# Padding the two tiles of the softmax sums from 48 to 256 bytes per partition

## The chip, the core and the metric

One core of a Trainium2 chip runs the whole program. The metric is the time of one execution on the device in microseconds; smaller is better. The engines are TensorE (PE in the rows, its weight loads PEld), VectorE (DVE), ScalarE (ACT), GpSimd (POOL) and SyncE (SP), which here issues nearly all DMA transfers. SBUF is the on-chip memory of 128 partitions; a tile takes the same range of bytes in each of its partitions, so one number, the byte at which it starts, says where it lies.

## What is computed

Attention in which a query sees only the keys of its own hash bucket, and two multilayer blocks on its output, in single precision:

```
q_bucket = bits(q @ proj > 0);  k_bucket = bits(k @ proj > 0)     # 6 bits each
scores = where(q_bucket == k_bucket, q @ k.T / 8, -1e9)           # 2 x 8 heads, 768 x 768, depth 64
p = exp(scores - max(scores));  attn = (p / (sum(p) + 1e-9)) @ v
x = attn as 1536 tokens x 512
h = max(x @ w1, x @ w2, x @ w3) @ w_out                           # 512 -> 768 -> 512
g = where(y >= 1, y, where(y <= -1, 0, (y + 1)**2 / 4)), y = h @ w_in
out = g @ w_out2                                                  # 512 -> 2048 -> 512
```

## The kernel before

**Attention** (to about 235 us) goes through 96 tiles of 128 queries. For each tile TensorE makes scores of 768 keys (lines 374 and 377: `lo` by `qa`, then `hi` by `qb`), VectorE copies them to a tile `p` and finds the extreme (384), ScalarE takes the exponential in place and writes the row sums to one column of the tile `sums` (396), TensorE transposes the six blocks of `p` (404, against the identity `ident`), ScalarE or VectorE copies them out to `pt` (413), and after three tiles TensorE multiplies `pt` by the values `vr` (422). A pair of heads has one tile `sums` of 12 columns; two such tiles take turns (`bufs=2` of the pool `nm`). At the end of a pair VectorE turns the sums into reciprocals (465, 466), TensorE transposes them (469), and the normalised result is written to `x_hl` as a high and a low part.

**The multilayer blocks** (from about 235 us, with their first few products already inside attention) are three loops over products of 128 x 128 weights with 512 columns, each made of three passes of high and low parts: `l1` and the loop behind it (both through the helper `mm3`, line 708), `l3` (line 708 too) and `l4` (line 835). `l3` and `l4` take turns, twelve products of one and twelve of the other. A weight slice is loaded by DMA to `wr`, taken apart by ScalarE, VectorE and GpSimd by way of `wg` and `wg2`, and put into one of seven buffers that are used in rotation: five named `w` and, once attention has given back its memory, two named `wx`.

In a product one operand is loaded into the array first (the stationary one, `lhsT`) and the other is streamed through it (the moving one, `rhs`). At line 708 the weights `w` or `wx` are stationary and `x_hl` or `hh` moves; at line 835 `g` is stationary and the weights `w` or `wx` move. In attention, `qa`, `qb`, `p` and `vr` are stationary and `lo`, `hi`, `ident` and `pt` move.

**Where the tiles lie.** Pools are placed one behind the other in the order in which they are opened, a tile's size being rounded up to 32 bytes. The pool `nm` opens behind the constants, `x_hl`, the weight buffers and the tiles `h`, and its first two tiles are `sums`. They take 48 bytes each, so 64 with rounding, and 128 together. Everything ahead of them ends at a multiple of 256; everything behind them that has a size of a multiple of 256 therefore begins 128 bytes past one:

| tiles | start of the first, bytes | past a multiple of 256 |
|---|---|---|
| `ident`, `x_hl`, `wr`, `wg`, `wg2`, `w`, `h` | 18432 (`ident`), 18944 (`x_hl`), 84480 (`w`) | 0 |
| `sums` | 111104 and 111168 | 0 and 64 |
| `u`, `uc`, `uo`, `rt`, `rb`, `xr`, `r` | 111232 (`u`) | 128 |
| `hi`, `lo`, `qa`, `qb`, `vr`, `p`, `pt` | 136320 (`hi`) | 128 |
| `wx`, `hh`, `acc`, `g` and the `r` of the multilayer blocks | 130176 (`wx`), 138368 (`hh`), 162944 (`g`) | 128 |
| `nm` (four of 4 bytes), `z` | 205440, 205568 | 128 to 224, 0 |
| `pj_st`, two parts | 16960, 17392 | 64, 240 |

The slices that products and transposes take of `x_hl`, `w`, `wx`, `hh`, `g`, `p`, `pt`, `vr` and the like begin a multiple of 256 bytes into their tile, so a slice lies past a multiple of 256 as its tile does.

Of the kernel before, what the change touches and what calls it, by code (L numbers as in the profile page):

```python
# [8 lines left out]
F32 = mybir.dt.float32  # L9
# [10 lines left out]
NK = S // 128  # L20
# [90 lines left out]
def lsh_attention_moe_kernel(  # L111
# [23 lines left out]
    nm_p = ctx.enter_context(tc.tile_pool(name="nm", bufs=2))  # L135
# [113 lines left out]
    def attention(mlp_steps):  # L249
        with ExitStack() as ax, ExitStack() as sx:  # L250
# [10 lines left out]
            head, pair, tl, grp = {}, {}, {}, {}  # L261
# [128 lines left out]
            def t_exp(n):  # L390
                h, t = divmod(n, NK)
                if n % (2 * NK) == 0:
                    pair[h // 2] = dict(sums=nm_p.tile([128, 2 * NK], F32, tag="sums", name="sums"))
                p = tl[n]["p"]
                c = (h % 2) * NK + t
                nc.scalar.activation(  # L396
                    out=p, in_=p, func=ACTF.Exp, scale=-1.0, bias=tl[n]["nm"],
                    accum_out=pair[h // 2]["sums"][:, c:c + 1],
                )
# [199 lines left out]
            def tile_tasks(n):  # L599
                h, t = divmod(n, NK)  # L600
                g, r = divmod(n, 3)
                sp, pp = place("s", 1), place("p", 2)
                tb = [place(f"t{i}", 1) for i in range(2)]
                if n % (2 * NK) == 0:
                    sums_p[h // 2] = place("sums", 1)
                if r == 0:
                    pt_p_[g] = place("pt", 1)
                qk = task("PE", 0.75, n, t_qk, n, after=ready[h], takes=[sp], leaves=[h_place[h]])
                mx = task("DVE", 0.97, n, t_max, n, after=[qk], takes=[pp], leaves=[sp])
                ex = task("ACT", 1.06, n, t_exp, n, after=[mx], takes=[sums_p[h // 2]] if n % (2 * NK) == 0 else [], lag=0.1)  # L610
                exps[n] = ex
                outs, tr = [], None
                for half in range(2):
                    tr = task("PE", 0.325, n - 4, t_tr, n, half, after=[ex, tr], takes=[tb[half]], leaves=[pp], lag=0.1)
                    cp = task("ACT", 0.48, n - 2, t_out, n, half, nc.scalar.copy, after=[tr], takes=[pt_p_[g]] if r == 0 and half == 0 else [], leaves=[tb[half]])
                    work.also("DVE", 0.55, lambda a=(n, half, nc.vector.tensor_copy): t_out(*a), cp)
                    outs += [cp]
                return outs
# [34 lines left out]
            for n in range(NT_):  # L653
                h, t = divmod(n, NK)
# [259 lines left out]
```

## Time and profile before

| | us |
|---|---|
| median of 3 runs (704.96 to 705.01) | 704.96 |
| the profiled execution, its own time | 704.98 |
| its span, first to last instruction | 703.2 |
| TensorE busy in the span | 695.2 |
| VectorE, ScalarE, GpSimd busy | 455.5, 374.0, 282.7 |

The profiled execution is 0.02 us from the median and its span 1.8 us shorter than its time. Products overlap in TensorE's pipeline: the duration of one (near 390 ns for 512 columns) is longer than the distance from one to the next, so the pace is read from how many fall in a stretch. A stretch's count has every product of which any part lies in it.

### The profile page before, as it was taken

The numbers are of one execution on the slowest core, as the hardware profiler recorded it, in microseconds if no ns is written. First come the engines' busy times: TensorE is split into PE (matmuls) and PEld (weight loads), VectorE is DVE, ScalarE is ACT, GpSimd is POOL, SyncE is SP. The second block draws the span as 40 slices with busy tenths as digits, with TensorE's granted clock in tenths as the row PEclk, the third lists the DMA queues.
The fourth block names the chain that finished last, engine by engine and source line by source line (L and its number), as shares of the span: only waits on it lengthen the run. The fifth ranks groups of instructions, "written<-read, shape, count | busy, mean of one in ns | idle before, by whom it ended". The sixth has DMA issues, their size and how long they took to land.

```text
span 703.2 us, 9982 instructions
## 1 busy us (share of the span) xinstructions
PE 695.2 (99%) x3548; PEld 553.9 (79%) x3548; DVE 455.5 (65%) x696; ACT 374.0 (53%) x733; POOL 282.7 (40%) x262
## 2 busy tenths in 40 slices
PE   8999999999999999999999999999999999999998
PEld 6777777777777688888888888888888888888886
DVE  6646555666655486775444355765888888888844
ACT  4788898888888423332321233665544444444430
POOL 3555646647523034442332022444344344344330
PEclk9999999999999999999999999999999999999999
DMA  5655557546511222221111022120111122111004
GB/s 164 162 149 151 132 145 202 139 121 167 132 46 45 95 91 90 90 91 52 56 49 54 31 89 90 47 75 31 60 61 61 60 66 84 61 61 60 31 0 180
DMA packets 25658, 62.78 MB, mean 89 GB/s; under 512 B 4085, under 2 KB 9813, under 8 KB 25609
## 3 DMA queue, kind: packets, MB, share of 16 engines
q1 hardware_dynamic: 25576, 62.15, 29.2%
q8 instruction: 28, 0.46, 0.3%
q14 instruction: 22, 0.17, 0.1%
q0 software_dynamic: 32, 0.00, 0.0%
HBM read 42.07 MB, written 3.19 MB: 64 GB/s over the span
## 4 chain that ended last, share of the span: by engine, by line
PE 97%; DVE 1%; issue 0%; DMA 0%; ACT 0%; DVEq 0%; ACTq 0%
PE b L708 47%; PE b L835 19%; PE u_ps L422 10%; PE t_ps L404 9%; PE s_ps L374 5%; PE s_ps L377 5%; PE pj_ps L337 2%; DMA r<-in_kq 0%; DVE p L384 0%; DVE lo L302 0%; DVE qb L344 0%; DVE qa L331 0%; DVE pt L413 0%; PE pj_ps L469 0%; ACT pt L413 0%
## 5 line engine op out<-in xcount | busy, mean ns | idle before, releaser
L708 PE MATMUL b<-x_hl,w 128*128 128x512 f32 (+1 forms) x900 | 203.1, 382 | 0.0
L708 PEld LDWEIGHTS b<-x_hl,w 128*128 128x128 f32 x900 | 164.0, 188 | 34.2 <-issue 0.6
L384 DVE TENSOR_SCALAR_CACHE_REDUCE p<-s_ps 128x768 f32<-128x768 f32 x96 | 91.1, 955 | 43.7 <-PE s_ps L377 32.4
L735 POOL TENSOR_TENSOR g<-r,g 128x512 fp32r<-128x512 f32 x48 | 62.6, 1306 | 125.6 <-ACT g L734 125.6
L835 PE MATMUL b<-w,g 128*128 128x512 f32 (+1 forms) x438 | 108.4, 392 | 0.0
L219 POOL TENSOR_TENSOR w<-wg,w 128x512 fp32r<-128x512 f32 (+1 forms) x42 | 59.4, 1414 | 96.7 <-ACT w L213 80.8
L835 PEld LDWEIGHTS b<-w,g 128*128 128x128 f32 x438 | 81.9, 189 | 18.7
L396 ACT ACTIVATE p<-p,nm 128x768 f32<-128x768 f32 x96 | 89.8, 937 | 9.0 <-DVE p L384 8.5
L192 DVE SCALAR_TENSOR_TENSOR wg<-wg,wr 128x512 f32<-128x512 f32 (+1 forms) x58 | 66.1, 1140 | 36.2 <-ACT wg L190 35.4
L213 ACT CAST w<-wg 128x512 fp32r<-128x512 f32 (+1 forms) x42 | 25.4, 605 | 115.6 <-DVE wg L205 115.6
L708 PE MATMUL b<-x_hl,wx 128*128 128x512 f32 x360 | 86.1, 395 | 0.0
L404 PEld LDWEIGHTS t_ps<-ident,p 128*128 128x128 f32 x576 | 66.5, 140 | 22.7 <-ACT p L396 11.5
L404 PE MATMUL t_ps<-ident,p 128*128 128x128 f32 x576 | 82.1, 276 | 1.1 <-DVE pt L413 0.9
L708 PEld LDWEIGHTS b<-x_hl,wx 128*128 128x128 f32 x360 | 67.9, 189 | 15.8
L413 ACT COPY pt<-t_ps 128x384 f32<-128x384 f32 x158 | 69.5, 480 | 18.2 <-PE t_ps L404 16.3
L374 PE MATMUL s_ps<-lo,qa 128*128 128x384 f32 x192 | 72.3, 377 | 1.0 <-DVE p L384 0.9
L422 PE MATMUL u_ps<-pt,vr 128*64 128x384 f32 x384 | 69.6, 495 | 0.2 <-ACT pt L413 0.2
L377 PE MATMUL s_ps<-hi,qb 76*128 76x384 f32 x192 | 65.3, 340 | 0.2 <-DVE hi L331 0.2
L815 DVE SCALAR_TENSOR_TENSOR r<-r,b 128x512 f32<-128x512 f32 x48 | 33.0, 687 | 48.2 <-ACT r L814 47.8
L842 DVE TENSOR_TENSOR acc<-b,acc 128x512 f32<-128x512 f32 (+1 forms) x85 | 56.5, 676 | 8.0 <-PE b L835 8.0
L813 ACT ACTIVATE r<-b,half_sb 128x512 f32<-128x512 f32 x48 | 32.9, 686 | 46.1 <-PE b L708 40.8
L197 DVE TENSOR_SCALAR wg<-wg 128x512 int32<-128x512 int32 (+1 forms) x58 | 53.9, 929 | 2.8
(80 smaller groups left out, 847.5 us busy)
## 6 DMA issues: line engine op xcount, KB each, us to landing
wr<-in_w SPq DMA_DIRECT2D x50, 512.0 KB, 3.1
r<-in_kq SPq DMA_DIRECT2D x15, 384.0 KB, 3.9
vr<-in_v SPq DMA_DIRECT2D x16, 192.0 KB
rb<-d SPq DMA_DIRECT2D x16, 192.0 KB, 3.3
wr<-in_w SPq DMA_DIRECT2D x8, 384.0 KB, 2.8
qa<-hi SPq DMA_DIRECT2D x15, 192.0 KB
qb<-hi SPq DMA_DIRECT2D x15, 192.0 KB, 4.0
qa<-lo SPq DMA_DIRECT2D x15, 192.0 KB, 2.7
```

What stands on the lines that cost most here:

```text
L192: nc.vector.scalar_tensor_tensor(out=f32(g), in0=f32(g), scalar=TINY_SQ, in1=f32(high), op0=ALU.is_ge, op1=ALU.mult)
L219: nc.gpsimd.tensor_tensor(out=w[:, 1, 0:cols], in0=f32(g2), in1=f32(w[:, 0, 0:cols]), op=ALU.subtract)
L374: nc.tensor.matmul(out=o, lhsT=hd["qa"][:, qs], rhs=hd["lo"][:, ks], start=True, stop=False)
L377: nc.tensor.matmul(out=o, lhsT=hd["qb"][0:76, qs], rhs=hd["hi"][0:76, ks], start=False, stop=True)
L384: nc.vector.tensor_scalar(out=p.rearrange("p (a k) -> p a k", a=2), in0=s_ps[n % 2][:, :, 0:HALF], scalar1=MASKED, scalar2=MASKED, op0=ALU ...
L396: nc.scalar.activation(out=p, in_=p, func=ACTF.Exp, scale=-1.0, bias=tl[n]["nm"], accum_out=pair[h // 2]["sums"][:, c:c + 1],)
L404: nc.tensor.transpose(out=t_ps[half][:, j * 128:(j + 1) * 128], in_=tl[n]["p"][:, kt * 128:(kt + 1) * 128], identity=ident,)
L413: copy(out=grp[g][:, 3 * half:3 * half + 3, r * 128:(r + 1) * 128], in_=t_ps[half][:, 0:HALF].rearrange("p (j q) -> p j q", j=3),)
L422: nc.tensor.matmul(out=u_ps[rows, 0:HALF], lhsT=vr[:, kt, :], rhs=grp[g][:, kt, :], start=(i == 0), stop=(i == 2),)
L708: nc.tensor.matmul(out=outp, lhsT=w_[a], rhs=x_[b_], start=(i == 0 and jj == 0), stop=(i == n - 1 and jj == 2),)
L735: nc.gpsimd.tensor_tensor(out=dst[:, 1, cs], in0=src, in1=f32(dst[:, 0, cs]), op=ALU.subtract)
L835: nc.tensor.matmul(out=pb[:, cs], lhsT=gs[f][:, a, tsl], rhs=wt[:, b_, cs], start=(n == 0), stop=(n == len(terms) - 1),)
```

## The change

The tile `sums` is allocated with 64 columns in place of 12 (256 bytes in place of 48), and its first 12 columns are used as before. No instruction is added, removed or moved on any engine; only addresses differ. The second `sums` starts at 111360, and each tile behind it moves up by 384 bytes: `u` to 111616, `wx` to 130560, `hi` to 136704, `hh` to 138752, `g` to 163328, all multiples of 256. `nm` then lies 0 to 96 bytes past a multiple of 256 and `z` 128; `pj_st` and the other constants, ahead of the pool, stay where they are.

```diff
--- before.py
+++ after.py
@@ -390,7 +390,7 @@
             def t_exp(n):
                 h, t = divmod(n, NK)
                 if n % (2 * NK) == 0:
-                    pair[h // 2] = dict(sums=nm_p.tile([128, 2 * NK], F32, tag="sums", name="sums"))
+                    pair[h // 2] = dict(sums=nm_p.tile([128, 64], F32, tag="sums", name="sums")[:, 0:2 * NK])
                 p = tl[n]["p"]
                 c = (h % 2) * NK + t
                 nc.scalar.activation(
```

## Rows read from the trace of the kernel before

**Rows 1.** The page: busy time by engine, and the chain that ended last, by line.

```profile
PE 695.2 (99%) x3548; PEld 553.9 (79%) x3548; DVE 455.5 (65%) x696; ACT 374.0 (53%) x733; POOL 282.7 (40%) x262
...
PE b L708 47%; PE b L835 19%; PE u_ps L422 10%; PE t_ps L404 9%; PE s_ps L374 5%; PE s_ps L377 5%; PE pj_ps L337 2%; DMA r<-in_kq 0%; DVE p L384 0%; DVE lo L302 0%; DVE qb L344 0%; DVE qa L331 0%; DVE pt L413 0%; PE pj_ps L469 0%; ACT pt L413 0%
```

**Rows 2.** Groups by line and shape (busy us, mean ns | idle), TensorE's matmuls, whole span.

```profile
L708 PE MATMUL b<-x_hl,w 128*128 128x512 f32 x828 | 195.3, 391 | 0.0
L835 PE MATMUL b<-w,g 128*128 128x512 f32 x426 | 107.0, 395 | 0.0
...
L708 PE MATMUL b<-x_hl,wx 128*128 128x512 f32 x360 | 86.1, 395 | 0.0
...
L708 PE MATMUL b<-hh,w 128*128 128x512 f32 x162 | 38.7, 395 | 0.0
L835 PE MATMUL b<-wx,g 128*128 128x512 f32 x144 | 37.9, 391 | 0.0
...
L708 PE MATMUL b<-hh,wx 128*128 128x512 f32 x54 | 13.2, 392 | 0.0
...
L708 PE MATMUL b<-x_hl,w 128*128 128x256 f32 x72 | 9.4, 283 | 0.0
...
L835 PE MATMUL b<-w,g 128*128 128x256 f32 x12 | 1.6, 282 | 0.0
```

**Rows 3.** Stretches: busy us of PE, PEld, DVE, ACT, POOL; granted clock; DMA share, GB/s.

```profile
300.00:330.00 30.00, 30.00 (x134) 24.83 (x134) 19.24 (x26) 9.49 (x17) 11.17 (x8) 1.00 0.24 84
410.00:450.00 40.00, 40.00 (x174) 32.46 (x173) 24.71 (x34) 18.23 (x31) 10.61 (x9) 1.00 0.23 79
490.00:508.00 18.00, 18.00 (x81) 14.90 (x80) 15.16 (x20) 7.79 (x13) 7.96 (x6) 1.00 0.16 58
234.89:453.17 218.28, 218.28 (x986) 180.31 (x986) 130.93 (x185) 72.32 (x130) 69.62 (x53) 1.00 0.21 72
453.19:680.31 227.12, 227.12 (x985) 185.26 (x985) 177.81 (x214) 109.83 (x186) 93.38 (x68) 1.00 0.16 56
120.00:235.00 115.00, 114.18 (x740) 84.28 (x739) 66.31 (x136) 96.37 (x214) 53.78 (x61) 1.00 0.41 108
```

**Rows 4.** Groups by line, 300 to 330 us, then 410 to 450 us, TensorE.

```profile
L708 PE MATMUL b<-x_hl,w 128*128 128x512 f32 x134 | 30.5, 389 | 0.0
...
L708 PE MATMUL b<-hh,w 128*128 128x512 f32 x103 | 24.1, 395 | 0.0
L708 PE MATMUL b<-x_hl,wx 128*128 128x512 f32 x71 | 16.7, 395 | 0.0
```

**Rows 5.** Groups by line, 234.89 to 453.17 us, then from 680.33 us, TensorE.

```profile
L708 PE MATMUL b<-x_hl,wx 128*128 128x512 f32 x216 | 50.7, 395 | 0.0
...
L835 PE MATMUL b<-w,g 128*128 128x512 f32 x72 | 17.2, 395 | 0.0
```

**Rows 6.** The chain in order of time (start us, us, what).

```profile
127.59 0.66 PE t_ps L404 x6
...
491.96 2.73 PE b L835 x12
...
602.42 2.79 PE b L835 x12
```

**Rows 7.** Instructions in order of time (start us, us), first 11 us, TensorE.

```profile
8.31 0.94 PE L265 MATMUL t_ps<-warm 128*128 128x256 bf16 x7
...
9.71 0.61 PE L265 MATMUL t_ps<-warm 128*128 128x256 bf16 x4
```

**Rows 8.** Groups by line, ScalarE, whole span.

```profile
L213 ACT CAST w<-wg 128x512 fp32r<-128x512 f32 x36 | 22.3, 621 | 100.0 <-DVE wg L205 100.0
...
L213 ACT CAST wx<-wg 128x512 fp32r<-128x512 f32 x14 | 8.7, 622 | 41.1 <-DVE wg L205 41.1
```

**Rows 9.** The page's DMA issues (count, KB each, median us from issue to landing).

```profile
r<-in_kq SPq DMA_DIRECT2D x15, 384.0 KB, 3.9
...
wr<-in_w SPq DMA_DIRECT2D x8, 384.0 KB, 2.8
```

## The prediction

> **What bounds the kernel now.** I read the page first. TensorE is busy 695.2 of 703.2 us, and the seven TensorE lines at the head of the chain that ended last hold 97% of the span; two of them, 708 and 835 of the multilayer blocks, hold 66% [rows 1]. So an edit that only moves addresses can change the time in two ways: by the pace of TensorE's own products, or by delaying something so much that TensorE begins to wait. In the multilayer blocks TensorE has no idle time in front of a product [rows 2], so there each nanosecond of pace is a nanosecond of the end.
>
> Then I sorted the products of 512 columns by the names of their two operands and set the places of the tiles beside them. Six pairs occur [rows 2]. In three of them both operands lie equally far past a multiple of 256 bytes: `x_hl` with `w` (0 and 0), `g` with `wx` (128 and 128), `hh` with `wx` (128 and 128). They take 391, 391 and 392 ns. In the other three one operand lies at 0 and the other at 128: `g` with `w`, `x_hl` with `wx`, `hh` with `w`. They take 395 ns, all three. That is a table with both factors crossed: `x_hl` is fast with `w` and slow with `wx`, `hh` the other way round, and so is `g`. Neither the line, the buffer, nor being at 128 explains it; only whether the two operands agree does. The durations overlap, so I checked the pace in stretches that hold one kind alone. From 300 to 330 us there is only `x_hl` with `w` [rows 4]: 134 products in 30.00 us plus the 0.389 us by which the first reaches in, 30.389 / 134 = 226.8 ns each [rows 3]. From 410 to 450 us there are only `hh` with `w` and `x_hl` with `wx` [rows 4]: 40.395 / 174 = 232.2 ns [rows 3]. [...] Disagreeing operands cost **5.4 ns per product**. The chain says the same where `l3` and `l4` take turns: a piece of twelve takes 2.73 us at 492 us, in a run of such pieces where both operands agree, and 2.79 us at 602 us where they don't [rows 6], 5 ns each.
>
> **The change part by part.** The edit adds no instruction and moves none. It puts `wx`, `hh`, `g` and all of attention's tiles at a multiple of 256; `x_hl`, `w` and `ident` are there already. After it all six pairs are (0, 0), like `x_hl` with `w` now.
>
> *Layers of line 708 from 234.89 to 453.17 us.* Slow pairs: 216 of `x_hl` with `wx` [rows 5] and all 162 of `hh` with `w` [rows 2], 378 products. 378 x 5.4 ns = **2.0 us**. Where two kinds follow each other some neighbours pay too: the mean of `hh` with `wx`, which stands between slow ones, is 392 and not 389 [rows 2, 4]. 54 such at 0 to 5 ns are 0 to 0.3 us; I take **0.2**.
>
> *`l3` and `l4`, 453.19 to 680.31 us.* 985 products in 227.12 us [rows 3], that is (227.12 + 0.39) / 985 = 231.0 ns. At 226.8 ns they take 985 x 0.2268 - 0.39 = 223.0 us: **4.1 us** less. The other end is the pace of the agreeing pieces of this stage itself, 2.73 / 12 = 227.5 ns [rows 6], which gives 223.7 us, 3.4 less. I take 226.8, since those pieces go back and forth between two operands at 0 and two at 128, and after the change nothing does.
>
> *The last products*, from 680.33 us: 72 of `g` with `w` at 512 columns [rows 5] x 5.4 ns = **0.4 us**. The halves of 256 columns show nothing: 283 ns agreeing, 282 disagreeing [rows 2].
>
> *Attention's products.* `lo` with `qa`, `hi` with `qb`, `pt` with `vr` all agree before and after: 0. The 576 transposes go from 128 against 0 to agreement. A piece of six on the chain takes 0.66 us [rows 6], 110 ns each; warm-up products of 256 columns, which read one and the same tile twice, are (0.94 - 0.61) / 3 = 110 ns apart [rows 7], and a transpose of this type seems to take as long as 256 such columns. No excess is to be seen, as with 256 columns above; I take 0. Rounding of these rows leaves 2 ns, 576 x 2 = 1.2 us, as the bound of a gain; a loss is excluded by the rows of pairs that agree, which are nowhere the slower ones. The hash products read `pj_st` at 64 and 240, which no padding of `sums` touches; against operands at 0 in place of 128 one part may lose what another wins, and 93 products x 5.4 ns = 0.5 us bounds it either way. I take 0.
>
> *Other engines and DMA.* They run behind TensorE, with slack. ScalarE's cast takes 621 ns to `w` at 0 and 622 to `wx` at 128 [rows 8], so I take 0 for the engines. Of the transfers, only the first load stands before TensorE's first real work; half of a head goes to `r`, at 128 now. A load of 384 KB takes 3.9 us to `r` and 2.8 us to `wr`, which lies at 0 [rows 9]; the first runs in denser traffic, so all of that difference is more than the place can make, and for the half it is 0.55 us. I take 0, with 0.55 us as the bound of a gain. [...] No row of before shows one load at both places.
>
> **Sum.** 2.0 + 0.2 + 4.1 + 0.4 = 6.7 us off the profiled 704.98: **698.3 us**, 0.95% faster. That execution is 0.02 us from the median, so the median is forecast at the same value.
>
> **The rivals.**
>
> *A, no change (705.0 us).* The difference between pairs belongs to something that goes with the buffers and not with 128 bytes, such as who writes them at that time, or stationary and moving operands don't meet in SBUF at all. For it: both kinds differ by little, and the high counts rest on few buffers. Against it: the crossed table, with the same buffer fast in one pair and slow in another. [...] That it could still fall out so: 0.10.
>
> *B, part of it (700.4 us).* TensorE gets faster and the next engine sets the pace. In `l3` and `l4` that would be VectorE: 15.16 of 18.00 us busy from 490 to 508 us, 84% [rows 3]. But there TensorE runs at the fast pace already and waits for nobody: 18.39 / 81 = 227.0 ns. It decides only where TensorE finds no free bank or no finished weight slice, and no row shows that now. Half of the 4.1 us of `l3` and `l4` lost gives 700.4. Chance 0.08.
>
> *C, slower (707.5 us).* Attention's tiles leave 128 and join the tiles at 0 that the weight pipeline, `x_hl` and `ident` use. If keeping engines on different places is what lets them run beside each other, exponentials and copies slow down. ScalarE is busy 96.37 of 115.00 us from 120 to 235 us, 84% [rows 3]; it decides from 19% longer operations (115.00 / 96.37). To end slower it must eat more than the 6.7 us; at 24% ScalarE needs 96.37 x 1.24 = 119.5 us for those 115, 3.9% over, 9.2 us of attention's 235, and the time is 707.5. Against it: the cast above is as long at 0 among tiles at 0 as at 128, and from 300 to 330 us, where nearly everything in use is at 0, TensorE has its best pace. Chance 0.05.
>
> **How the numbers follow.** The forecast has 0.77, A 0.10, B 0.08, C 0.05. Range: below, 698.3 less 1.2 for the transposes and 0.55 for the first load, 696.5; above, B's 700.4 and 0.5 for the hash products, 700.9, which takes in the 227.5 ns end (0.7). That leaves out A, C and a little at the edges, 0.2. A measurement of this kernel can tell about 0.2%, 1.4 us, from no change: the forecast and B are faster (0.85), A is the same (0.10), C is slower (0.05).
>
> **What would show it.** In the profile after, all six pairs of 512 columns at 389 or 390 ns; about 226.8 ns apart in any stretch, so 2.72 us for each twelve of line 835 and of line 708 alike; the multilayer blocks beginning within half a microsecond of 234.9 us and lasting 458.3 in place of 465 us. Attention's transposes 110 ns apart as now. I am wrong if the pairs still differ, if all stay at 395, if products begin to wait in the multilayer blocks, or if these begin later than 235.5 us.

## The result, and the profile after

The changed kernel takes **698.18 us** (median of 4 runs, 698.14 to 698.26) against 704.96: a ratio of 0.9904, 95% interval 0.9888 to 0.9920. The profiled execution has a span of 696.4 us, 6.8 less than before. The forecast was 698.3.

The first view is again the groups by line and shape, TensorE's products of 512 columns over the whole span (busy us, mean ns | idle before), the answer to [rows 2]:

```profile
L708 PE MATMUL b<-x_hl,w 128*128 128x512 f32 x828 | 194.2, 389 | 0.0
L835 PE MATMUL b<-w,g 128*128 128x512 f32 x426 | 104.5, 389 | 0.0
L708 PE MATMUL b<-x_hl,wx 128*128 128x512 f32 x360 | 84.0, 389 | 0.0
...
L708 PE MATMUL b<-hh,w 128*128 128x512 f32 x162 | 37.7, 389 | 0.0
L835 PE MATMUL b<-wx,g 128*128 128x512 f32 x144 | 37.5, 389 | 0.0
...
L708 PE MATMUL b<-hh,wx 128*128 128x512 f32 x54 | 13.1, 389 | 0.0
```

Six pairs, one number. The 395 of three of them is gone, and so are the 391 and 392 of the pairs that agreed already but had slow neighbours.

The second view is the chain in order of time (start us, us, what), the answer to [rows 6]; the stage of line 708, two pieces where `l3` and `l4` take turns, and the last stage:

```profile
235.13 215.80 PE b L708 x984
...
592.38 2.72 PE b L835 x12
595.10 2.72 PE b L708 x12
...
673.98 19.12 PE b L835 x90
```

The third is the busy time by stretch (PE, PEld, DVE, ACT, POOL; granted clock; DMA share, GB/s), the answer to [rows 3]:

```profile
410.00:450.00 40.00, 40.00 (x178) 33.14 (x177) 25.41 (x35) 20.19 (x35) 12.63 (x10) 1.00 0.24 79
...
235.13:450.92 215.79, 215.79 (x986) 179.90 (x986) 130.50 (x185) 72.32 (x130) 69.29 (x53) 1.00 0.22 73
450.95:673.97 223.02, 223.02 (x985) 184.66 (x985) 177.70 (x214) 109.58 (x186) 93.35 (x68) 1.00 0.18 57
```

The same 986 products of the first layers take 215.79 in place of 218.28 us, the same 985 of `l3` and `l4` 223.02 in place of 227.12. TensorE is busy for all of both stretches, at the same granted clock, 1.00. From 410 to 450 us 178 products fit where 174 did: (40 + 0.389) / 178 = 226.9 ns.

### The profile page after: what moved, and what is told of

It is laid out like the page before. It is cut to its first block, busy times and chain, and to the rows that moved or that the text cites. A ratio compares the mean times of both kernels' runs of the same rounds, so it can differ in the third digit from the quotient of the medians.

```text
span 696.4 us, 9982 instructions
## 1 busy us (share of the span) xinstructions
PE 688.5 (99%) x3548; PEld 553.2 (79%) x3548; DVE 454.7 (65%) x696; ACT 373.9 (54%) x733; POOL 282.4 (41%) x262
## 4 chain that ended last, share of the span: by engine, by line
PE 97%; DVE 1%; issue 0%; DMA 0%; ACT 0%; DVEq 0%; ACTq 0%
PE b L708 47%; PE b L835 19%; PE u_ps L422 10%; PE t_ps L404 10%; PE s_ps L374 5%; PE s_ps L377 5%; PE pj_ps L337 2%; DMA r<-in_kq 0%; DVE p L384 0%; DVE lo L302 0%; DVE qb L344 0%; DVE qa L331 0%; DVE pt L413 0%; PE pj_ps L469 0%; ACT pt L413 0%
## 5 line engine op out<-in xcount | busy, mean ns | idle before, releaser
L835 PE MATMUL b<-w,g 128*128 128x512 f32 (+1 forms) x438 | 105.9, 386 | 0.0
L708 PE MATMUL b<-x_hl,wx 128*128 128x512 f32 x360 | 84.0, 389 | 0.0
```

The source lines that it names most:

```text
L708: nc.tensor.matmul(out=outp, lhsT=w_[a], rhs=x_[b_], start=(i == 0 and jj == 0), stop=(i == n - 1 and jj == 2),)
L835: nc.tensor.matmul(out=pb[:, cs], lhsT=gs[f][:, a, tsl], rhs=wt[:, b_, cs], start=(n == 0), stop=(n == len(terms) - 1),)
```

## The experiments

Twelve kernels, all built on the changed one; the edits move addresses alone, unless said otherwise, and none changes what is computed. The cuts of code show the main line of an edit, with `...` where something is left out. A tile's "place" is its start modulo 256; two operands "agree" when their places are equal. Where a view merges products into pieces, the text goes by the start and the end of each single product in the trace; the profile models the ends, so a split of a few ns between neighbours is less sure than their sum.

| run | edit | us | ratio to before, 95% |
|---|---|---|---|
| e1_all_128 | every large tile at 128 | 698.14 | 0.9902 (0.9885 to 0.9918) |
| e2_pad_128 | `sums` of 128 bytes, the rest at 0 | 698.06 | 0.9903 (0.9888 to 0.9918) |
| e3_att_128 | attention alone at 128 | 697.84 | 0.9898 (0.9883 to 0.9913) |
| e4_g_128 | `g`, `acc` and the `r` beside them alone at 128 | 703.31 | 0.9976 (0.9966 to 0.9986) |
| e5_off_64 | what lies behind `sums` at 64 | 705.25 | 1.0006 (0.9996 to 1.0015) |
| e6_off_32 | the same at 32 | 705.41 | 1.0007 (0.9997 to 1.0016) |
| e7_off_192 | the same at 192 | 702.66 | 0.9967 (0.9955 to 0.9980) |
| e8_low_128 | all low parts at 128, high parts at 0 | 706.56 | 1.0023 (1.0014 to 1.0033) |
| e9_kk_128 | every second block of `w`, `wx` and `x_hl` at 128 | 704.36 | 0.9992 (0.9983 to 1.0002) |
| e10_off_96 | what lies behind `sums` at 96 | 706.85 | 1.0028 (1.0018 to 1.0038) |
| e11_hash | e3 with `pj_st` at 128 too | 697.62 | 0.9896 (0.9882 to 0.9911) |
| e12_wlow_128 | low parts of `w`, `wx` at 128 | 705.48 | 1.0007 (0.9997 to 1.0017) |

**Is it a multiple of 256, or agreement?** The change puts the large tiles at multiples of 256. The prediction says that only agreement counts.

```diff
-    warm = const.tile([128, CH], BF16, name="warm")
+    const.tile([128, 32], F32, name="pad"); warm = const.tile([128, CH], BF16, name="warm")
```

> The changed kernel with 128 bytes more in front of every large tile: ident, x_hl, w, wx, hh, g and attention's tiles all lie 128 past a multiple of 256. If only agreement of the stationary with the moving operand counts, all six pairs stay at 389 ns, 226.8 ns apart, and the time is 698.2 us. If lying at a multiple of 256 is what counts, all products of 512 columns (1974) run at 232.2 ns or slower: 1974 x 5.4 ns = 10.7 us more, 708.9 us.

Measured 698.14. No large tile lies at a multiple of 256, and the time is that of the changed kernel. All six pairs take 389 ns, and twelve products of either line 2.72 us, as in this piece of the chain:

```profile
600.45 2.72 PE b L708 x12
```

Agreement counts; the multiple doesn't.

**Do the padded tiles themselves matter?**

```diff
-                    ... nm_p.tile([128, 64], F32, tag="sums", name="sums")[:, 0:2 * NK])
+                    ... nm_p.tile([128, 32], F32, tag="sums", name="sums")[:, 0:2 * NK])
```

> The sums tiles have 128 bytes each in place of 256, so the second one lies 128 past a multiple of 256, and every tile behind them at a multiple of 256 as in the changed kernel. If the sums themselves don't matter and only what lies behind them does: 698.2 us. If the place of the sums tiles has a part in the gain (through the row sums' writes, the reciprocals, the eight transposes of sums): above 698.2, up to 705.0.

Measured 698.06: tiles of half the size give the whole gain, with the second `sums` at 128. The tiles of the sums only pushed the rest. This run also says that 256 is the measure and not 512: in the changed kernel all operands of the multilayer blocks lie whole multiples of 512 bytes apart, and here, where everything behind the sums lies 256 bytes lower, `x_hl` and `wx` are 111360 bytes apart, 217.5 times 512, at the same pace: the layers of line 708 take 215.81 us here and 215.80 in the changed kernel.

**Does attention take part?**

```diff
-            raw_p = ax.enter_context(tc.tile_pool(name="raw", bufs=2))
+            raw_p = ax.enter_context(tc.tile_pool(name="raw", bufs=2)); raw_p.tile([128, 32], F32, name="pad", bufs=1)
```

> The changed kernel with attention's tiles alone (r, hi, lo, qa, qb, vr, p, pt) put back to 128 past a multiple of 256; all operands of the multilayer blocks at 0. If attention had no part in the gain, as the prediction's sum has it: 698.2 us, with the blocks beginning within 0.5 us of where they begin in the changed kernel. If attention gained through transposes or loads: up to 1.7 us more, 699.9.

Measured 697.84, 0.3 us *under* the changed kernel. The blocks begin at 234.87 us, where they began before the change (234.89), against 235.13 in the changed kernel. So attention has no part in the gain. That its move to 0 costs the 0.26 us is not shown: in e1 attention lies at 128 too, its first load lands 0.08 us earlier than in the changed kernel (2.33 and 2.41 us), and yet the blocks begin at 235.05. The transposes, whose operands disagree here and agree in the changed kernel, have the same mean in both, 276 ns.

A follow-up on the hash products, the one pair in attention that no run so far had made agree:

```diff
-    pj_st = const.tile([128, 2, 108], F32R, name="pj_st")
+    const.tile([128, 16], F32, name="pad"); pj_st = const.tile([128, 2, 128], F32R, name="pj_st")[:, :, 0:108]; const.tile([128, 8], F32, name="pad2")
```

> The run with attention alone at 128 past a multiple of 256 (697.84 us), and in it the two parts of pj_st placed at 128 past a multiple of 256 as well, so that the hash products' operands agree too. If they pay for disagreeing as the products of 512 columns do: 93 x 2 to 5 ns = 0.2 to 0.5 us less, 697.3 to 697.6. If they pay nothing: 697.8.

Measured 697.62, 0.22 under e3, at the small end of what paying for disagreement would give. The chains of e3 and of this run begin the blocks here:

```profile
234.87 215.82 PE b L708 x984
```

```profile
234.56 215.81 PE b L708 x984
```

That is 0.31 us in attention, but most of it is not in the hash products. The distances from start to start between hash products that follow each other sum to 0.09 us less than in e3, and those between score products that follow each other to 0.18 us less, though the score products' own operands agree in both runs. By the ends the hash products gain nothing. So that they pay for disagreeing is not shown. This run has the lowest median of all, but 0.08% under the changed kernel is less than these measurements can tell.

**Does the price hold line by line?**

```diff
-                acc = g_p.tile([128, NT // 128, DM], F32, name="acc")
+                g_p.tile([128, 32], F32, name="pad"); acc = g_p.tile([128, NT // 128, DM], F32, name="acc")
```

> The changed kernel with only acc, g and the r of the last blocks at 128 past a multiple of 256. Only line 835 then has operands that disagree (g with w and g with wx, 570 products of 512 columns). If each disagreeing product costs 5.4 ns: 570 x 5.4 = 3.1 us more, 701.3 us (to 701.5 with neighbours at the seams), line 835 at 395 ns and line 708 at 389. If the cost were one of the wx and hh buffers, none of which moved: 698.2.

Measured 703.31: 5.1 us, where 3.1 was expected. Two pieces of its chain:

```profile
600.88 2.80 PE b L835 x12
603.68 2.76 PE b L708 x12
```

Line 835 is slow, as expected. But line 708, whose operands all agree, takes 2.76 in place of 2.72 us for twelve when it stands between slow pieces. In the single ends of the trace the twelfth of such a piece ends 233.7 ns after the eleventh, while the weights of the first disagreeing product are loaded; and after a slow piece the first seven are uneven (226 to 235 ns) before they settle at 226.7. So a product can pay for its neighbours. From start to start, line 835 costs 3.5 us more than in the changed kernel, 6.2 ns a product and not 5.4, and line 708 beside it 1.5 us. The rival, that the cost sits in the buffers `wx` and `hh`, falls.

**Which difference counts?** The runs at 64 and 192 give the sums another size (first cut). The run at 32 leaves them as in the changed kernel and puts 32 bytes in front of them in their pool `nm` (second cut); the run at 96 makes both edits.

```diff
-                    ... nm_p.tile([128, 64], F32, tag="sums", ...
+                    ... nm_p.tile([128, 40], F32, tag="sums", ...    # 24 for the run at 192
```

```diff
-    nm_p = ctx.enter_context(tc.tile_pool(name="nm", bufs=2))
+    nm_p = ctx.enter_context(tc.tile_pool(name="nm", bufs=2)); nm_p.tile([128, 8], F32, name="pad", bufs=1)
```

> All tiles behind the sums lie 64 past a multiple of 256, those ahead of them at 0: the pairs that disagreed by 128 before now disagree by 64. If only the half of a 256-byte stretch counts (the 128s place of the address): 698.2 us, all pairs at 389 ns. If any difference counts: 705.0 us, the three pairs at 395.

> As the run before, with 32 in place of 64. If only the half of a 256-byte stretch counts: 698.2 us. If any difference of the starts counts: 705.0 us. If the cost grows with the distance: between these, some 700 (a quarter of 6.8 us over 698.2).

> As the run before, with 192 in place of 32. If the 128s place of the address alone counts: 705.0 us, since 192 lies in the other half. If the distance to the nearest multiple of 256 counts (64 here), the same time as at 64.

> All tiles behind the sums 96 past a multiple of 256, those ahead of them at 0. If what counts is the moving operand's start less the stationary one's, modulo 256 (the runs at 32, 64, 128 and 192 gave 233 ns at 224, 192 and 32, 232 at 128, 229 to 230 at 64), hh with w stands at 96 and comes to lie between 229 and 232.5 ns, x_hl with wx and w with g stand at 160 and come to lie at 232.5 to 233.5: some 705 us. If the size of the difference alone counts, the three pairs are equal.

Measured 705.25, 705.41, 702.66 and 706.85. That one half of a 256-byte stretch counts against the other is wrong: 32 and 64 cost as much as 128 did. Nor does the distance to the nearest multiple decide: 64 and 192 differ by 2.6 us. The groups by line, the three disagreeing pairs of the run at 64, then of the run at 192, then of the run at 96:

```profile
L835 PE MATMUL b<-w,g 128*128 128x512 f32 x426 | 107.3, 395 | 0.0
L708 PE MATMUL b<-x_hl,wx 128*128 128x512 f32 x360 | 86.4, 395 | 0.0
L708 PE MATMUL b<-hh,w 128*128 128x512 f32 x162 | 38.1, 391 | 0.0
```

```profile
L835 PE MATMUL b<-w,g 128*128 128x512 f32 x426 | 106.1, 393 | 0.0
L708 PE MATMUL b<-x_hl,wx 128*128 128x512 f32 x360 | 85.1, 392 | 0.0
...
L708 PE MATMUL b<-hh,w 128*128 128x512 f32 x162 | 38.8, 395 | 0.0
```

```profile
L835 PE MATMUL b<-w,g 128*128 128x512 f32 x426 | 107.6, 396 | 0.0
L708 PE MATMUL b<-x_hl,wx 128*128 128x512 f32 x360 | 86.7, 397 | 0.0
L708 PE MATMUL b<-hh,w 128*128 128x512 f32 x162 | 38.8, 395 | 0.0
```

The first two are mirror images. In `hh` with `w` the moving operand is the shifted one, in the other two the stationary one. Take the moving start less the stationary start, modulo 256: at 64 the products take 391 to 393 ns, at 192 they take 395, whichever tile it is that moved. At 96 they take 395, at 160 396 to 397, at 128 (before) 395, and at 32 and 224 (the run at 32) 395 and 395 to 396. The expectation for the run at 96, that it lies between 64 and 128, missed: it is as slow as 128, and the run is 1.9 us slower than "some 705". In the profiled execution (707.28) some 0.6 us lie in attention: the blocks begin at 235.69 us, against 235.13 in the changed kernel. Only where all pairs stand at 0 do all take 389.

**Which weights meet which moving operand?** While a product streams, the weights of the next one are being loaded: in the traces of before and after, from 300 to 330 us, the load begins some 3 ns after the product's start and takes 188 ns. Three runs give products and their successors different places.

```diff
-        x_hl = x_p.tile([128, 2, 4, NT], F32R, name="x_hl")
+        x_hl = x_p.tile([128, 2, 4 * NT + 32], F32R, name="x_hl")[:, :, 0:4 * NT].rearrange("p a (k n) -> p a k n", k=4)
-            w = w_p.tile([128, 2, 512], F32R, tag="w", name="w", bufs=WEARLY)
+            w = w_p.tile([128, 2, 544], F32R, tag="w", name="w", bufs=WEARLY)[:, :, 0:512]
...
```

> The changed kernel with the low parts of w, wx, x_hl, hh and g (index 1) moved 128 bytes further, the high parts at a multiple of 256. The three passes are high-high, high-low, low-high: in two of three the stationary and the moving operand of the same product disagree, while the weights loaded for the next product always agree with the operand that moves meanwhile (next weights high, low, high against moving high, low, high). If a product's own two operands count: 2/3 of 1974 x 5.4 ns = 7.1 us more, 705.3 us. If it is the next weights being loaded while the current operand streams: no disagreement is left, 698.2 us.

Measured 706.56, 8.4 us more. That the next weights alone count is excluded; the sum is a fifth above that of a product's own operands (7.1). By the single ends from 300 to 330 us, the three passes end 234.2, 229.4 and 229.7 ns after the one before, where 226.7 is the pace of agreement. So the latest is the first pass, which agrees with its own weights and with the next ones (from each start to the next the three are 232.4, 229.2 and 231.7).

```diff
-                mm3(pb, [(wk(wt, kk), (x_hl[:, 0, kk, ts], x_hl[:, 1, kk, ts])) for kk in range(4)])
+                mm3(pb, [(wk(wt, kk, 160), (x_hl[:, 0, kk, ts], x_hl[:, 1, kk, ts])) for kk in range(4)])
...
```

> The changed kernel with every second 128-column block of the first and third layers' weights (w, wx) and every second block of x_hl moved 128 bytes further, both alike. Each product of line 708 on x_hl (1188 of 512 columns) then agrees with its own weights; in one of three the weights of the next product disagree with what moves now; in two of three the weights of the next but one do. If the product's own two operands count: 698.2 us. If the next weights count: 396 x 5.7 ns = 2.3 us more, 700.4. If the next but one: 792 x 5.7 ns = 4.5 us more, 702.7.

Measured 704.36, 6.2 us more, beyond all three. Every product here agrees with its own weights, and yet there are only 130 of them from 300 to 330 us, (30 + 0.395) / 130 = 233.8 ns each:

```profile
300.00:330.00 30.00, 30.00 (x130) 24.09 (x129) 17.76 (x25) 9.21 (x17) 10.76 (x8) 1.00 0.25 84
```

So a product's own operands alone are excluded too. To keep the blocks apart, the weights are written in four blocks each in this run; TensorE's busy time has no gap in the stretch. In `l3` the same pattern between agreeing pieces of line 835 costs less, 2.76 us for twelve.

```diff
-            w = w_p.tile([128, 2, 512], F32R, tag="w", name="w", bufs=WEARLY)
+            w = w_p.tile([128, 2, 544], F32R, tag="w", name="w", bufs=WEARLY)[:, :, 0:512]
-            w = w_state["more"].tile([128, 2, 512], F32R, tag="wx", name="wx", bufs=WBUFS - WEARLY)
+            w = w_state["more"].tile([128, 2, 544], F32R, tag="wx", name="wx", bufs=WBUFS - WEARLY)[:, :, 0:512]
```

> The changed kernel with the low parts of w and wx alone moved 128 bytes further; x_hl, hh and g stay at a multiple of 256 in both parts. One product of three disagrees (low weights by high moving at line 708, high g by low moving weights at line 835): 658 x 5.7 ns = 3.8 us more, 701.9 us, whichever pairing counts. Which of the three passes ends late tells the pairings apart at line 708: the third (its own weights are the low ones) if the product's own operands count, the second if the next weights do, the first if the next but one do.

Measured 705.48, 7.3 us more, twice the expectation, and the single ends say where. From 300 to 330 us, at line 708, the three passes end 226.2, 233.7 and 233.4 ns after the one before: the second, during which the disagreeing weights are loaded, *and* the third, which uses them. At line 835, where the shifted part moves and all stationary operands are at one place, one of three is late: 226.7, 232.5, 227.2. Here, then, a product pays some 6 to 7 ns if its own weights or the next ones disagree with what it streams. Two thirds of line 708's 1404 products and one third of line 835's 570 are 936 + 190 = 1126; 7.3 us / 1126 = 6.5 ns. In e8 the same rule gives two thirds of 1974, 8.4 us / 1316 = 6.4 ns. That fits the sum and not the passes: there the first pass agrees by this rule, and it is the latest. In e9 it gives one third of 1188, and the 6.2 us measured are more than twice what 396 x 6.5 ns = 2.6 us would be. So it is no rule for single products: of the three runs it fits e12 alone. As in e4, a disagreement seems to go on costing in products that agree. How, is not shown.

## Why the prediction was right

*The crossed table of pairs, and that only agreement counts.* Right. All six pairs are at 389 ns after, and e1 shows the gain without a single large tile at a multiple of 256. The rows of before held it already: two levels of a factor on either side, and stretches of one kind alone.

*Layers of line 708: 2.0 + 0.2 us.* Measured 218.28 - 215.80 = 2.5 us. From start to start, the 378 disagreeing products gave 2.24 us of it, 5.9 ns each, and those that agreed already 0.25. So the 0.2 for neighbours was right, and the 5.4 ns was a little too small: a count of products in a stretch can be off by one, and one in 174 is 1.3 ns.

*`l3` and `l4`: 4.1 us, to 223.0.* Measured 227.12 - 223.02 = 4.1. Taking the pace of the clean stretch and not the 2.73 us pieces of this stage itself was the right choice: twelve take 2.72. The whole-stage sum held the cost at the seams, which a count of disagreeing products times 5.4 ns leaves out: from start to start, 1.2 of the 4.1 us came from products that agreed already. e4, forecast by such a count, was short by 2.0 us, 1.5 for the neighbours and the rest for the price.

*The last products: 0.4 us.* Measured 19.55 - 19.12 = 0.43. The piece of the chain before:

```profile
680.32 19.55 PE b L835 x90
```

*Attention: 0.* Measured -0.24: the blocks begin at 235.13 and not at 234.89 us. It lies within the 0.5 us that bounded the hash products either way, but it is not theirs. From start to start, the distances between hash products that follow each other sum to 12.25 us before and 12.21 after, and those between score products that follow each other to 58.96 and 59.19. The run e1 has the hash operands 64 and 144 apart, as e3 and the kernel before have them, and still ends attention late, with 59.21 us between score products where e3 has 58.97:

```profile
235.05 215.79 PE b L708 x984
```

Why the score products, whose own operands agree in all four, lie further apart in two of them is not shown. The transposes' bound of 1.2 us was not needed.

*The sum.* 2.48 + 4.10 + 0.43 - 0.24 = 6.8 us, against 6.7. That the sum is so close is in part luck: the layers gained 0.3 us more than forecast, and attention lost nearly as much.

*Rival A* falls. The edits move addresses alone, and the pace goes with them: from 410 to 450 us a product takes 226.9 ns where the operands agree modulo 256 (178 products after, in e1 and in e4) and 230.8 to 232.2 where they don't (175 in e5 and e7, 174 before), with the granted clock at 1.00 and the DMA share at 0.23 or 0.24 in each of these runs. What makes the difference, no run shows. *Rival B* falls: VectorE is busy 177.70 of 223.02 us in `l3` and `l4`, and TensorE has no gap. *Rival C* falls: at 0 or at 128, attention takes the same within 0.3 us.

*The first load: 0.* It takes 2.41 us to a place at 0 and took 2.44 to 128; between the runs it is 2.26 (e2) to 2.41 at 0 and 2.33 (e1) to 2.42 (e3) at 128. A difference between the two places does not stand out from that scatter of 0.15 us, and the bound of 0.55 us was not needed.

## What to carry to other kernels

Where TensorE sets the end and its products follow each other without a gap, sort them by the names of their operands and compare the means before looking for waits: 4 to 6 ns of 390, in pairs that cross, were 6.8 us here. Place stationary and moving operands, and the slices taken from them, at the same distance past a multiple of 256 bytes; which distance made no difference here (698.18 us at 0, 698.14 at 128), and a small tile in the middle of a pool is enough to break it, as the two `sums` of 64 bytes each did. When a cost is counted product by product, add the seams: here the neighbours of slow products paid too, 1.2 of the 4.1 us of `l3` and `l4`. All this is shown for back-to-back products of 512 columns in this number type; the twelve halves of 256 columns of `g` with `w` took 282 ns before and after.

## What the runs showed that was not expected

The cost depends on the sign of the difference: with the moving operand 64 bytes past the stationary one a product takes 391 to 393 ns, with it 64 before (192) 395. It is there at every step tried, 32, 64, 96, 128, 160, 192 and 224 (391 to 397 ns), and absent only at 0 (389). And the rule for single products that fits e12 does not hold elsewhere: in e8 the pass that agrees with its own and the next weights is the latest, and e9 is slow in products that agree with their own weights, most of them with the next ones as well, by 7 ns each in the first layers and by less than half of that in `l3`. A fixed price for a pair does not describe that; what carries it over stays open.
